# One contiguous piece per weight slab, and an identity made by GpSimd: a layer norm feeding a spectral filter and a gated MLP

## The chip, the cores and the metric

The kernel runs on one core of a Trainium2 chip. The metric is device time in microseconds (us), the median of several runs. A profile comes from one further execution; its times are counted from its first instruction. Engines are called PE or TensorE (matrix products), DVE or VectorE, ACT or ScalarE, POOL or GpSimd, and SP or SyncE, which here issues all loads and stores ("SPq" in the profile is its issuing of them).

## The reference, cut to what matters

The input x has 2048 rows of 448 columns. It is normalised by row, and three things are added: x itself, a spectral filter of the normalised rows (a two-dimensional real FFT, a product with complex weights, the inverse), and an MLP whose gate passes only where it is positive.

```python
x = A_x                                   # 1 x 2048 x 448
xn = _layernorm(x, axis=-1)
X = rfft2(xn) * (w_r + 1j * w_i);  a = irfft2(X)
gate = xn @ W_gate; up = xn @ W_up        # 448 x 1792 each
h = gate * (gate > 0) * up
return x + a + h @ W_down                 # 1792 x 448
```

## The kernel before, in words

**Precision.** Float32 operands are split into two float16 parts, hi and lo, and a product is made of three passes (hi hi, hi lo, lo hi). For that, weights are first scaled by a power of two: ScalarE sums the squares of a slab (`w_sq`, line 194), GpSimd adds over the partitions (`w_sum`, line 197), VectorE makes the scale from the exponent in two instructions (`w_scale`, lines 200 and 204), ScalarE writes the hi part (`w_hi`, line 664) and VectorE the lo part (`w_lo`, line 668).

**Tiling.** The 2048 rows are 16 blocks of 128 (n2 from 0 to 15), taken as four chunks of four blocks in the order 0, 2, 1, 3. The 1792 hidden columns are 14 tiles f of 128, in groups of 5, 5 and 4. A unit "gu" makes gate and up of one tile for one chunk (lines 714 and 721), a unit "dn" the down projection of one group for one block (line 782). A slab (f, g) is the weight of tile f for gate (g = 0) or up (g = 1): 128 partitions of 4 x 128 float32. `load_w` (line 234) loads one slab, and eight slabs have room in SBUF at a time. Before, the array in DRAM is laid out (tile, partition, gate or up, 4, 128), so that a slab is 128 rows of 2,048 bytes, 4 KB apart.

**The opening.** The first part of the order is written out by hand, in the string `OPENING` (line 30): each token stands for a piece of work, and under `tc.manual_schedule` (line 1074) every engine does its instructions in this order. `lx` and `lw` load a block of x (line 228) and the next slab; `lid` loads the identity (line 1022), `lwd` a tile of the down weights (line 244); `st` makes a block's statistics (lines 256 and 259), `sqA`/`sqB` the standard deviations (ScalarE, line 267) and `rsA`/`rsB` their inverses (VectorE, lines 272 to 277); `xn` normalises (line 294); `hi` and `lo` split (lines 301 and 323); `cp` copies columns together on GpSimd (lines 307 and 308); `tpA` and `tpB` transpose on TensorE against the identity `id_t` (line 338), and `vev`/`aev` bring the result to SBUF on VectorE (line 346) or ScalarE (line 344). `warm` and `kw` are matrix products of zeros (line 1020) that keep TensorE busy; their operand is made by a MEMSET on GpSimd (line 1077). `hh`, `lh` and `hl` are the first product passes. All loads go through SyncE's queue in the order of the string. It begins `lx0 lx4 lw lid lw lx8 lx12 lw lw lw lw lx2`.

Only the transposes of the first chunk use the identity. Those of later chunks are DMA transposes (line 332).

**Behind the opening** the order isn't written out. The program gives every unit its side work: `sched` (line 976) sets slab work so many gu units ahead of its first use, and a list of FFT pieces with costs is drawn down by `run_bg`. The costs of VectorE pieces are in `V_US` (line 1088). The framework's scheduler then orders each engine by priorities and by modelled times (`schedule_with_timeline_sim`, line 1186), with anchors (`tc.issue_after`) that hold side work behind earlier units.

**The inverse transform** needs pairs of rows swapped between partitions; this is done by two DMAs each (`swap`, lines 547 and 548), on which VectorE waits at line 553.

## Time and profile before

| | us |
|---|---|
| median of 3 runs | 448.41 |
| the runs | 447.95, 448.41, 448.84 |
| span of the profiled execution | 446.9 |

For the profiled execution no other time than its span is listed.

Rows of a timeline read: start in us, duration in us (for x4 the whole stretch of four), engine, line, operation, output <- input, shape, count, and in brackets how long the engine had been idle before and what released it. Rows of groups read: the same names, then total busy us, mean ns of one, idle time before them and its releasers. Rows of the chain of waits read: start, duration, what was on the chain. A row of the table by stretches gives the window, its length, the busy time and count of each engine, the granted TensorE clock (1.00 is full), the DMA engines' mean busy share and the rate in GB/s.

### The profile page before, as it was taken

To read this page: it belongs to the slowest core of one execution; us is meant where nothing else is said; L and a number is where in the kernel's file an instruction comes from. 1 tells how busy PE (TensorE), PEld (TensorE's weight loads), DVE (VectorE), ACT (ScalarE), POOL (GpSimd) and SP (SyncE) were. 2 spreads that over 40 slices of the span, in tenths; PEclk is the share of its full clock that TensorE was granted. 3 is DMA by queue.
4 is the path that set the end of the run, shared out by engine and by line. 5 is a ranking of instruction groups with operands and counts; after the bars stand their busy time and mean duration, and the time that the engine had idled before them with its cause. 6 is when DMAs were issued, how large, how long until landed. Compare 5 with 4: busy or idle time off the path is not lost.

```text
span 446.9 us, 7057 instructions
## 1 busy us (share of the span) xinstructions
PE 437.4 (98%) x2618; PEld 217.6 (49%) x2618; DVE 373.0 (83%) x801; ACT 178.7 (40%) x365; POOL 35.5 (8%) x100
## 2 busy tenths in 40 slices
PE   7999999999999999999999999999999999999996
PEld 2543545444545444444444444444444456546564
DVE  5988696998859989899999999896997998656474
ACT  5886242451543666043224145434142242233230
POOL 2431031040000150000000010000000000000000
PEclk9999999999999999999999999999999999999999
DMA  7919976041001261431220021000001332121113
GB/s 243 362 38 266 359 243 118 1 94 38 0 14 61 96 219 37 129 103 64 82 77 11 1 83 54 0 13 0 14 0 42 106 96 74 54 76 53 64 43 123
DMA packets 36827, 39.66 MB, mean 89 GB/s; under 512 B 17799, under 2 KB 32185, under 8 KB 36793
## 3 DMA queue, kind: packets, MB, share of 16 engines
q1 hardware_dynamic: 36792, 39.21, 28.1%
q8 instruction: 20, 0.33, 0.3%
q14 instruction: 15, 0.11, 0.1%
HBM read 24.45 MB, written 3.67 MB: 63 GB/s over the span
## 4 chain that ended last, share of the span: by engine, by line
PE 84%; DVE 7%; DMA 4%; ACT 1%; issue 1%; POOL 1%; SPq 1%; DVEq 0%; ACTq 0%
PE gu L714 47%; PE dn L782 27%; PE gu L721 3%; PE fx L360 2%; PE fx L392 2%; DMA sw<-y 2%; PE fx L611 2%; PE fx L632 1%; DMA y<-in_xr 1%; DVE g L755 1%; DMA T<-tt 1%; DVE bst L256 1%; DVE wt L668 1%; DVE xy L788 1%; DVE y L553 1%
## 5 line engine op out<-in xcount | busy, mean ns | idle before, releaser
L714 PE MATMUL gu<-T,wt 128*128 128x512 f16 (+1 forms) x1140 | 256.1, 376 | 0.0
L714 PEld LDWEIGHTS <-wt 128*128 128x128 f16 x1140 | 108.6, 98 | 129.9 <-issue 9.3
L782 PE MATMUL dn<-wdt,h 128*128 128x448 f16 x672 | 136.4, 352 | 0.0
L782 PEld LDWEIGHTS <-h 128*128 128x128 f16 x672 | 64.8, 98 | 60.5
L751 ACT ACTIVATE g<-gu 128x512 f32<-128x512 f32 x56 | 33.2, 594 | 111.0 <-PE gu L721 75.3
L759 ACT ACTIVATE h<-g 128x512 f16<-128x512 f32 x56 | 35.0, 626 | 52.8 <-DVE g L755 52.7
L755 DVE SCALAR_TENSOR_TENSOR g<-gu,g 128x512 f32<-128x512 f32 x56 | 38.3, 684 | 10.3 <-ACT g L751 10.2
L788 DVE SCALAR_TENSOR_TENSOR xy<-dn,dsc,xy 128x448 f32<-128x448 f32 x48 | 32.5, 678 | 15.5 <-PE dn L782 15.3
L763 DVE TENSOR_TENSOR h<-g,h 128x512 f16<-128x512 f32 x56 | 38.2, 684 | 4.9 <-ACT h L759 4.8
L664 ACT ACTIVATE wt<-wst,wsc 128x512 f16<-128x512 f32 x28 | 19.1, 716 | 15.7 <-DVE wsc L204 15.7
L197 POOL PARTITION_ALL_REDUCE wm<-wm x15 | 7.9, 523 | 159.2 <-ACT junk L194 159.2
L668 DVE SCALAR_TENSOR_TENSOR wt<-wst,wsc,wt 128x512 f16<-128x512 f32 x28 | 20.4, 744 | 0.0
L637 DVE SCALAR_TENSOR_TENSOR xy<-fx,fsc,xy 128x448 f32<-128x448 f32 x16 | 10.8, 679 | 10.1 <-PE fx L632 10.1
L721 PE MATMUL gu<-T,wt 64*128 64x512 f16 x112 | 17.0, 381 | 1.7 <-DVE g L755 0.8
L399 DVE TENSOR_TENSOR y<-y 128x456 f32<-128x456 f32 x22 | 13.9, 630 | 4.7 <-DMA row<-y 4.5
L194 ACT ACTIVATE junk<-wst 128x512 bf16<-128x512 f32 x28 | 17.4, 622 | 0.3
L553 DVE TENSOR_TENSOR y<-y,sw 128x456 f32<-128x456 f32 x16 | 10.0, 626 | 8.5 <-DMA sw<-y 8.5
L595 ACT ACTIVATE vt<-y,fsc 128x912 f16<-128x912 f32 x8 | 8.4, 1052 | 20.7 <-PE fx L611 12.3
L618 ACT ACTIVATE wf<-fx 114x512 f16<-114x512 f32 x16 | 9.4, 587 | 17.2 <-PE fx L611 17.0
L398 DVE TENSOR_TENSOR y<-y 128x456 f32<-128x456 f32 x22 | 13.8, 626 | 0.2
L611 PEld LDWEIGHTS <-vt 128*128 128x128 f16 x192 | 12.0, 98 | 3.3
L611 PE MATMUL fx<-wf,vt 128*128 128x128 f16 x192 | 13.2, 219 | 0.0
(115 smaller groups left out, 430.6 us busy)
## 6 DMA issues: line engine op xcount, KB each, us to landing
sw<-y SPq DMA_DIRECT2D x32, 224.4 KB
wst<-in_wgu SPq DMA_DIRECT2D x28, 256.0 KB
wf<-in_wf SPq DMA_DIRECT2D x8, 456.0 KB
y<-in_xr SPq DMA_DIRECT2D x16, 224.0 KB
xy<-in_x SPq DMA_DIRECT2D x16, 224.0 KB
out<-xy SPq DMA_DIRECT2D x16, 224.0 KB
wdst<-in_wd SPq DMA_DIRECT2D x14, 224.0 KB
fm<-in_c_fm SPq DMA_DIRECT2D x8, 128.0 KB
```

The source lines that it names most:

```text
L194: A.activation(o, src, AF.Square, scale=SQ, accum_out=acc)
L611: P.matmul(o, v[:, h, w], m[:, c, :], start=(i == 0), stop=(i == 2), skip_group_check=True)
L664: A.activation(w[:, 0:4, :], wst[f, g], AF.Copy, scale=wsc[f, g])
L668: V.scalar_tensor_tensor(w[:, 4:8, :], st, sc, w[:, 0:4, :], op0=OP.mult, op1=OP.subtract)
L714: last["P"] = P.matmul(hps[f, q][:, g, cs], wt[f, g][:, a, :], Tq[q][:, b, cs], start=(start and i == 0), stop=(stop and i == len(seq) - 1 ...
L721: m = P.matmul(hps[f, q][:, g, 0:512], wt[f, g][rows, 7, :], Tq[q][rows, b, :], start=start, stop=not start).ins
L751: last["A"] = A.activation(g1s[f, q], hps[f, q][:, 0, :], AF.Relu, scale=2.0 ** -22).ins
L755: last["V"] = V.scalar_tensor_tensor(g1, hps[f, q][:, 1, :], 2.0 ** -22, g1, op0=OP.mult, op1=OP.mult).ins
L759: A.activation(ht[f, q][:, 0, :], g1s[f, q], AF.Copy)
L763: V.tensor_tensor(h[:, 1, :], g1s.pop((f, q)), h[:, 0, :], op=OP.subtract)
L782: last["P"] = P.matmul(ps[:, 0:D], ht[f, q][:, a, js], wdt[f][:, b, :], start=(i == 0), stop=(i == n - 1)).ins
L788: last["V"] = V.scalar_tensor_tensor(xy[:, n2, :], dps[n2][:, 0:D], dsc[:, g:g + 1], xy[:, n2, :], op0=OP.mult, op1=OP.add).ins
```

## The change

Three things are changed.

1. The gate and up weights are laid out in DRAM as (tile, gate or up, partition, 4, 128), so that each slab is one piece of 256 KB. The load reads the same bytes into the same place.
2. The identity isn't loaded. GpSimd makes it: a MEMSET of zeros and an `affine_select` that writes 1 where row and column are equal. Both stand behind the MEMSET of the warm-up tile. The token `lid` leaves the string, and the input `ident` leaves the program.
3. The pieces `rs` and `wsc` of the string are cut into their single VectorE instructions (`rsA.0` to `rsA.4`, `wscW0g0.0` and `.1`, and so on). They stand next to each other where the whole pieces stood, so apart from `lid` the order is the same. In the scheduled part `w_scale` becomes `w_exp` and `w_scale`, set in the same slot one after the other.

```diff
-lx0 lx4 lw lid lw lx8 lx12 lw lw lw lw lx2 lx10 lx6 lx14 lwd0 lwd1 lwd2 lwd3 lwd4 warm st0 st4 sqA rsA hi4
+lx0 lx4 lw lw lx8 lx12 lw lw lw lw lx2 lx10 lx6 lx14 lwd0 lwd1 lwd2 lwd3 lwd4 warm st0 st4 sqA rsA.0 rsA.1 rsA.2 rsA.3 rsA.4 hi4
...
     def load_w(f, g, eng=nc.sync):
         wst[f, g] = mt([128, 4, 128], F32, "wst", 8)
-        eng.dma_start(wst[f, g], wgu[f, :, g])
+        eng.dma_start(wst[f, g], wgu[f, g])
...
+    def w_exp(f, gs=(0, 1)):
+        half_exponent(eg[:, f, gs[0]:gs[-1] + 1], state["wm", f][:, 1, gs[0]:gs[-1] + 1])
+
     def w_scale(f, gs=(0, 1)):
         sc = mt([128, 2], F32, "wsc", 6)
-        e = eg[:, f, gs[0]:gs[-1] + 1]
-        half_exponent(e, state["wm", f][:, 1, gs[0]:gs[-1] + 1])
-        shift_exponent(sc[:, 0:len(gs)], e, -1, 188)
+        shift_exponent(sc[:, 0:len(gs)], eg[:, f, gs[0]:gs[-1] + 1], -1, 188)
...
         sched(gslot(s, 7), w_sum, f)
+        sched(gslot(s, 5), w_exp, f)
         sched(gslot(s, 5), w_scale, f)
...
-    pieces = {"lid": lambda: nc.sync.dma_start(id_t, ident), "lfd": lambda: nc.sync.dma_start(fd_t, c_fd),
+    pieces = {"lfd": lambda: nc.sync.dma_start(fd_t, c_fd),
...
         G.memset(warm, 0.0)
+        G.memset(id_t, 0.0)
+        G.affine_select(id_t, id_t, pattern=[[-1, 128]], compare_op=OP.not_equal, fill=1.0, base=0, channel_multiplier=1)
         wps = psum.tile([128, 512], F32, name="dn", bufs=2)
...
-    wgu = np.ascontiguousarray(np.stack([wtiles(B_W_gate), wtiles(B_W_up)], axis=2))
+    wgu = np.ascontiguousarray(np.stack([wtiles(B_W_gate), wtiles(B_W_up)], axis=1))
```

## The prediction

> **What bounds the kernel now.** I read the page first (busy shares, DMA packets), then a table of busy time by stretch, then the opening instruction by instruction with the release of each wait.

> ```profile
> span 446.9 us, 7057 instructions
> PE 437.4 (98%) x2618; PEld 217.6 (49%) x2618; DVE 373.0 (83%) x801; ACT 178.7 (40%) x365; POOL 35.5 (8%) x100
> ```

> TensorE is busy for 437.4 of 446.9 us, so a change that leaves its work alone can win only out of the other 9.5 us. The table shows where these lie (after the window and its length come each engine's busy time with its count of instructions, then granted clock, DMA share, GB/s):

> ```profile
> 0.00:7.50 7.50, 5.92 (x19) 2.13 (x19) 3.21 (x12) 3.04 (x6) 1.35 (x11) 1.00 0.67 203
> 7.50:13.60 6.10, 3.57 (x26) 1.69 (x27) 5.47 (x22) 4.97 (x14) 2.16 (x7) 1.00 1.01 356
> 13.60:19.30 5.70, 5.54 (x56) 4.72 (x56) 5.60 (x15) 5.44 (x12) 2.28 (x7) 1.00 1.02 369
> 19.30:366.00 346.70, 345.93 (x1882) 163.77 (x1883) 308.80 (x676) 143.61 (x303) 29.75 (x76) 1.00 0.27 81
> 366.00:400.00 34.00, 33.19 (x263) 18.81 (x260) 23.02 (x39) 8.75 (x14) 0.00 (x0) 1.00 0.23 74
> 400.00:443.20 43.20, 43.20 (x378) 26.46 (x376) 26.17 (x39) 12.87 (x21) 0.00 (x0) 1.00 0.17 63
> 443.20:446.90 3.70, 0.06 (x1) 0.00 (x0) 0.68 (x1) 0.00 (x0) 0.00 (x0) 1.00 0.32 121
> ```

> From 13.6 us TensorE stands for 0.16 us to 19.3, 0.77 us to 366, 0.81 us to 400, and not at all to 443.2; then one last piece and a store take 3.7 us. The granted clock is 1.00 throughout. The kernel is an opening of 13.6 us and then TensorE's own work. Whatever makes the first product pass start earlier arrives at the end almost whole; whatever only speeds a load in the middle arrives nowhere. Everything turns on the opening, and here are its rows:

> ```profile
> 0.96 0.52 POOL L1077 MEMSET warm<- 128x512 f16 x1
> 2.14 0.43 SPq L1022 DMA_DIRECT2D id_t<-in_ident  x1
> 2.62 0.43 SPq L234 DMA_DIRECT2D wst<-in_wgu  x1
> 3.09 0.91 SPq L228 DMA_DIRECT2D y<-in_xr  x2
> 6.90 0.61 ACT L194 ACTIVATE junk<-wst 128x512 bf16<-128x512 f32 x1
> 7.06 0.22 POOL L307 COPY tt<-tt 128x48 f16<-128x48 f16 x1 [5.57 <-ACT tt L301]
> 7.51 0.74 ACT L301 ACTIVATE tt<-y,rs 128x448 f16<-128x448 f32 x1
> 7.85 0.63 DVE L256 BATCH_NORM_STATS2 bst<-y 128x6 f32<-128x448 f32 x1 [0.80 <-DMA y<-in_xr]
> 8.32 0.51 PE L338 MATMUL fx<-id_t,tt 128*128 128x128 f16 x6 [0.85 <-ACT tt L301]
> 9.46 0.29 ACT L267 ACTIVATE rs<-mv,eps 128x2 f32<-128x2 f32 x1 [0.58 <-DVE mv L259]
> 9.92 0.45 PE L338 MATMUL fx<-id_t,tt 128*128 128x128 f16 x5 [0.88 <-DVE tt L323]
> 12.03 0.45 PE L338 MATMUL fx<-id_t,tt 128*128 128x128 f16 x5 [0.36 <-DVE tt L323]
> 13.12 1.01 DVE L346 COPY T<-fx 128x384 f16<-128x384 f16 x3
> 13.62 0.33 PE L338 MATMUL fx<-id_t,tt 128*128 128x128 f16 x3 [0.48 <-ACT wt L664]
> ```

> One wait on a load stands in this chain: at 7.85 VectorE had stood 0.80 us for the third block of x (lx8). From there it is busy for 5.47 of the 6.10 us to 13.6, and TensorE and ScalarE wait for it (0.88 and 0.36 us for the low halves, 0.58 us for the statistics). The transposes themselves never wait for the identity: the first, at 8.32, was released by ScalarE's high half. And no row says that ScalarE's first sum of squares (6.90) waited for weights: it stands behind other ScalarE work.

> **The change part by part.** *The identity's load goes.* SyncE issues it at 2.14 in its order, and the next issue starts at 2.62: 0.48 us of SyncE, with the loads of W0g1, lx8, lx12 and all others behind it. The awaited lx8 is the second of these. How much earlier does it land? Two bounds, from the load's size and from the rate in the stretch in which it moves:

> ```profile
> id_t<-in_ident SPq DMA_DIRECT2D x1, 32.0 KB
> 4.00:5.00 1.00, 1.00 (x4) 0.37 (x3) 0.86 (x3) 0.07 (x1) 0.00 (x0) 1.00 0.67 164
> ```

> If the DMA engines were saturated, only the identity's bytes would go: 32.8 kB at the 203 GB/s of the first window is 0.16 us. If the pace is set by issuing, the whole slot goes: 0.48 us. From 4 to 5 us, after these issues and before lx8 has landed, the engines are busy for only 0.67 of the time at 164 GB/s, so they were short of work and not of bandwidth; that is nearer to the second bound. I take 0.45 us. The most that any earlier landing can give is the whole wait, 0.80 us: then VectorE is bound by its own order.

> Does 0.45 us pass down the chain? VectorE's pieces behind lx8 (statistics, low half, weight scale, second normalisation factor, evictions) follow each other closely, and their other inputs come from work that is not behind the load: the high half ends at 7.51 + 0.74 = 8.25, and the low half made from it is wanted by the transpose at 9.92, 0.45 earlier still over 1 us behind it. ScalarE has 0.58 us of slack at 9.46, more than 0.45. The transposes at 9.92 and 12.03 wait for VectorE and move with it, and with them the evictions at 13.12 and TensorE's start at 13.62. From there TensorE stands for so little that the shift reaches 443.2 and the last store.

> *The identity is made on GpSimd.* Two instructions more, behind the warm-up tile's MEMSET, which ends at 0.96 + 0.52 = 1.48. Their nearest rows:

> ```profile
> L313 POOL COPY tt<-tt 128x64 f16<-128x64 f16 x16 | 5.6, 349 | 0.0
> L197 POOL PARTITION_ALL_REDUCE wm<-wm x15 | 7.9, 523 | 159.2 <-ACT junk L194 159.2
> L488 POOL MEMSET sw<- 1x912 f32 x6 | 5.1, 850 | 0.2
> L284 POOL MEMSET tt<- 128x32 f16 x4 | 0.3, 124 | 0.3 <-POOLq L1178 0.3
> ```

> The MEMSET of 128 columns is a quarter of the warm-up tile's 0.52 us, so 0.13. The select has no row; it lies between a short MEMSET (0.12) and the longest mean of any GpSimd group, 0.85. I take the all-reduce's 0.52, as it too is more than a plain move. Together 0.65 us (0.25 to 0.98), from 1.48 to 2.13. GpSimd's next work is the copy at 7.06, after 5.57 us of idling: 4.93 us of cover. The warm-up matmuls wait for the MEMSET ahead of the two and do not move. Cost: nothing. If the cover were gone, the price would be the delay of the first transpose past 8.32, less the 0.43 us that TensorE would still wait before 9.92 (0.88 - 0.45).

> [...]

> *The weights lie in one piece.* The page and the tables say what each of the 28 loads does now:

> ```profile
> DMA packets 36827, 39.66 MB, mean 89 GB/s; under 512 B 17799, under 2 KB 32185, under 8 KB 36793
> wst<-in_wgu SPq DMA_DIRECT2D x28, 256.0 KB
> 13.00:14.00 1.00, 0.52 (x6) 0.39 (x6) 1.00 (x4) 1.00 (x2) 0.00 (x0) 1.00 1.06 402
> 9.12 3.60 SPq L244 DMA_DIRECT2D wdst<-in_wd  x5
> 155.05 1.01 SPq L234 DMA_DIRECT2D wst<-in_wgu  x2
> 156.50:157.50 1.00, 1.00 (x7) 0.23 (x6) 0.00 (x0) 0.17 (x2) 0.00 (x0) 1.00 0.98 367
> ```

> A load moves 128 rows of 2,048 B, now 4 KB apart, afterwards end to end. 28 x 128 = 3,584 packets of that size, with the 1,024 of the spectral weights (8 x 128 rows of 3.6 KB), make 4,608, which is the number of packets from 2 to 8 KB (36793 - 32185). So each row is one packet now. The down weights lie end to end already (rows of 1,792 B), and no packet between 2 and 8 KB is left over for them: they are not merged across partitions, so I expect the same 2,048 B packets afterwards. Nor does the pitch cost rate: from 13 to 14 us, behind their issue at 9.12, down weights move at 402 GB/s with a DMA share of 1.06; from 156.5 to 157.5 us two gate and up loads, issued at 155.05 and alone, move at 367 with a share of 0.98. Divided by the share that is 379 and 374, equal within 2%. I book nothing. Bounds: from no gain to the rest of lx8's wait, 0.80 - 0.45 = 0.35 us, as two of these loads are ahead of lx8; nothing more, as no other wait on them stands in the opening's rows.

> *The split pieces.* The normalisation factor and the scale are cut into single VectorE instructions, but the written order has them in the same sequence; only the identity's token is missing. In the scheduled part the scale's two instructions become two entries of the same slot with the same planned cost. Zero.

> The sum: 446.9 - 0.45 + 0 + 0 = 446.45 us of span. The page gives no time of its own for the profiled execution beside its span; the median of the runs, 448.41, lies 1.5 us above it, and I keep that distance: 447.96 us. What one measurement here can tell from no change is about 0.2%, 0.9 us; the forecast, -0.10%, is within it.

> **The rivals.** *Nothing arrives.* lx8 was late for a slow first transfer, not for its place in the queue, and VectorE waits as before: 448.4. For it: the DMA share from 7.5 us on is 1.01. Against it: the idle engines at 4 to 5 us.

> *The contiguous loads are faster.* The whole wait of 0.80 us goes: 447.6. For it: the early rate is 356 GB/s between 7.5 and 13.6, where weights move among others, below the later 402. Against it: the equal rates above. Still within the limit. [...]

> *The scheduled part is drawn anew, and better.* Past the opening the order on each engine is not written out: the scheduler makes it from modelled times, which change with the dropped load and the two new instructions. TensorE's 0.77 + 0.81 us could shrink, with the opening's 0.45 at most 2.0 us: 446.4, and about 447.0 for half of it.

> *The scheduled part is drawn anew, and worse.* This is the one that ends slower. Its place is the inverse transform's partition swaps between 366 and 400 us, where the chain of waits runs over VectorE and two loads:

> ```profile
> 380.45 4.33 DMA sw<-y
> 392.25 4.94 DMA sw<-y
> DVE y L553 <- DMA sw<-y: 8.5, 3, 4.3
> ```

> If a swap is issued later, behind another piece of VectorE's work, VectorE stands for a further part of such a landing, and TensorE with it once its down-projection work laid there (33.19 busy of 34.00) is used up. Half a landing, 2.3 us, less the opening's 0.45 gives 450.3; a delay of over 1.35 us on TensorE (0.45 + 0.9) makes it measurably slower. Against it: the anchors of the units are unchanged, and a uniform shift leaves an order as it is.

> *The identity comes late*, if the select took over 6.6 us (1.48 + 0.13 to 8.25): for 9 us the transpose is 2.4 us late, of which 0.43 is covered: 447.96 + 1.97 = 449.9.

> **How the numbers follow.** Forecast, the shift alone: 0.52. Nothing arrives: 0.10. Faster loads: 0.05. Drawn better: 0.18. Drawn worse: 0.12. Late identity: 0.03. Faster by over 0.2% (below 447.5) takes the better order and a little of the forecast's edge and of the faster loads: 0.21. Slower (above 449.3) takes the worse order and most of the last: 0.14. Within: 0.65. The range 446.8 to 449.2 holds the unknown costs (447.6 to 448.25 for the load's bounds), the half gain of a better order, and the small losses of a worse one, and leaves out about 2 in 10.

> **What would show it.** In the profile of the changed kernel: no id_t load; the next weight load's issue near 2.15; two more GpSimd rows that end near 2.1; the 0.80 us wait at 7.85 down to about 0.35, and TensorE's triple at 13.62 near 13.2; 2,048 B packets as before (128 under 512 B fewer) and the same rates; TensorE's standing from 13 us on near 1.7 us. It would be wrong if the wait stays, if a GpSimd row or a gap without a row reaches 7 us, or if the standing after 19 us changes by more than the opening does; the last would say that the order decides.

## The result and the profile after

The changed kernel takes 458.88 us (median of 4 runs, 458.8 to 459.55) against 448.4 us before: a ratio of 1.0236, 95% interval 1.0223 to 1.0249. The prediction was 447.96 us (446.8 to 449.2). The change costs 10.5 us.

The page of the changed kernel, its span and its first row of engines:

```profile
span 457.1 us, 7061 instructions
PE 440.8 (96%) x2618; PEld 219.2 (48%) x2618; DVE 373.4 (82%) x801; ACT 178.9 (39%) x365; POOL 36.1 (8%) x102
```

The span is 10.2 us longer, with 3.4 us more of TensorE's busy time for the same 2618 products, and two more GpSimd instructions. The table by stretches of the changed kernel (columns as before: engines' busy time and counts, granted clock, DMA share, GB/s) says where:

```profile
0.00:10.14 10.14, 7.12 (x19) 2.60 (x20) 5.36 (x18) 5.03 (x11) 1.43 (x12) 1.00 0.78 252
10.14:18.93 8.79, 0.94 (x11) 0.64 (x11) 0.37 (x4) 0.30 (x2) 1.12 (x6) 0.73 0.85 314
18.93:24.00 5.07, 5.07 (x20) 2.53 (x21) 4.67 (x18) 3.97 (x8) 2.39 (x8) 0.50 0.00 0
24.00:40.00 16.00, 15.73 (x104) 8.86 (x103) 13.72 (x37) 13.97 (x31) 3.35 (x14) 0.99 0.34 100
40.00:366.00 326.00, 324.97 (x1754) 153.65 (x1752) 288.84 (x630) 129.47 (x274) 27.77 (x67) 1.00 0.27 80
366.00:400.00 34.00, 34.00 (x257) 18.95 (x256) 28.10 (x50) 11.07 (x17) 0.00 (x0) 1.00 0.25 81
```

From 10.14 to 18.93 us hardly anything computes: TensorE 0.94 us, VectorE 0.37, ScalarE 0.30, GpSimd 1.12. Then TensorE works for 5.07 us at a granted clock of 0.50. From 24 to 400 us it stands for 0.27 + 1.03 + 0 = 1.3 us, no more than before (0.77 + 0.81 us from 19.3 to 400). Nearly the whole loss lies in the opening. Its timeline in the changed kernel (start, duration, engine, line, what, and the idle time ahead with its releaser; the lines of helpers are 3 to 10 lower than before):

```profile
0.96 0.52 POOL L1077 MEMSET warm<- 128x512 f16 x1
1.42 0.20 POOL L1078 MEMSET id_t<- 128x128 f16 x1
7.93 0.63 DVE L246 BATCH_NORM_STATS2 bst<-y 128x6 f32<-128x448 f32 x1 [0.84 <-DMA y<-in_xr]
9.81 0.28 POOL L1079 TENSOR_SCALAR_AFFINE_SELECT id_t<-id_t 128x128 f16<-128x128 f16 x1 [8.18 <-issue]
10.06 0.21 POOL L302 COPY tt<-tt 128x48 f16<-128x48 f16 x1
10.14 0.50 PE L333 MATMUL fx<-id_t,tt 128*128 128x128 f16 x6 [1.48 <-POOL id_t L1079]
18.13 0.40 POOL L187 PARTITION_ALL_REDUCE wm<-wm  x1 [7.67 <-issue]
18.41 0.28 POOL L302 COPY tt<-tt 128x48 f16<-128x48 f16 x1
18.56 0.15 DVE L190 TENSOR_SCALAR eg<-wm 128x1 uint32<-128x1 uint32 x1 [8.39 <-POOL wm L187]
18.58 0.30 POOL L303 COPY tt<-tt 128x64 f16<-128x64 f16 x1
18.93 0.29 PE L333 MATMUL fx<-id_t,tt 128*128 128x128 f16 x1 [7.85 <-POOL tt L303]
19.01 2.77 PE L1017 MATMUL dn<-warm 128*128 128x512 f16 x6
23.71 1.16 PE L710 MATMUL gu<-T,wt 128*128 128x256 f16 x6
```

The two brackets with "issue" on GpSimd are the result. The select itself takes 0.28 us, less than I had put down. But GpSimd is silent for 8.18 us ahead of it and for 7.67 us ahead of the first all-reduce, and in neither case waits for anything that the timeline shows: the select has no other producer than the MEMSET in front of it, and the sum of squares that the all-reduce reads was there at 7.46 + 0.19 = 7.65 (ScalarE, line 184). "issue" as a releaser is how a row says that time went by without a row. Everything else follows: the identity is there at 10.1 instead of ahead of 8.3, the first weight scale at 18.6 instead of near 10, the second block's columns, which GpSimd copies for the transposes, at 18.9 (18.58 + 0.30). VectorE waited 8.39 us and TensorE 7.85 us for GpSimd. In the kernel before, the second block's copy and the first weight scale read:

```profile
8.48 0.24 POOL L308 COPY tt<-tt 128x64 f16<-128x64 f16 x1
9.92 0.14 DVE L200 TENSOR_SCALAR eg<-wm 128x1 uint32<-128x1 uint32 x1
```

The timeline leaves out an entry that a view of one source line (`--source`) has: a MODIFY_POOL_CONFIG on GpSimd's sequencer (POOLq), for the line of the select and for that of the all-reduce, about where each silence begins (1.62 and 10.46 us). These rows read: line, queue, operation, count, shortest, median and longest time in ns, first and last start in us.

```profile
L1079 POOLq MODIFY_POOL_CONFIG  x2: 11/11/11, 1.6 to 1.7; - x2
L187 POOLq MODIFY_POOL_CONFIG  x2: 3/3/3, 10.7 to 10.7; - x2
```

The entry itself takes 3 to 11 ns. From 1.7 us to the select at 9.81, and from 10.7 to the all-reduce at 18.13, GpSimd has no row.

The kernel before has the second of these entries too, ahead of its first all-reduce, and yet no silence stood there; its row says that it waited 0.25 us for ScalarE's sum of squares:

```profile
L197 POOLq MODIFY_POOL_CONFIG  x2: 11/11/11, 7.5 to 7.5; - x2
7.70 0.39 POOL L197 PARTITION_ALL_REDUCE wm<-wm  x1 [0.25 <-ACT junk L194]
```

So the entry alone isn't the cost. But the trace of before already held a sign, at 7.5 us, that more goes with GpSimd's first all-reduce than its row in the timeline.

Two of the profiles below, of the layout alone and of the select that nobody reads, were taken in an execution in which TensorE was slower (spans of 1,628.8 and 1,628.7 us, and 5.20 us for the six warm-up products that took 1.46 us before); from them only rows of DMA and GpSimd are used, and such executions are left out of the times.

### The profile page after: what moved, and what is told of

It is laid out like the page before. It is cut to its first block, busy times and chain, and to the rows that moved or that the text cites. A ratio compares the mean times of both kernels' runs of the same rounds, so it can differ in the third digit from the quotient of the medians.

```text
span 457.1 us, 7061 instructions
## 1 busy us (share of the span) xinstructions
PE 440.8 (96%) x2618; PEld 219.2 (48%) x2618; DVE 373.4 (82%) x801; ACT 178.9 (39%) x365; POOL 36.1 (8%) x102
## 4 chain that ended last, share of the span: by engine, by line
PE 84%; DVE 6%; issue 5%; DMA 3%; ACT 1%; POOL 1%; SPq 0%; DVEq 0%; ACTq 0%; POOLq 0%
PE gu L710 46%; PE dn L778 26%; PE gu L717 3%; PE fx L355 2%; PE fx L387 2%; DMA sw<-y 2%; PE fx L606 2%; PE fx L627 1%; PE dn L1017 1%; DMA T<-tt 1%; DVE g L751 1%; DVE wt L664 1%; DVE xy L784 1%; DVE y L548 1%; DVE y L549 0%
## 5 line engine op out<-in xcount | busy, mean ns | idle before, releaser
L751 DVE SCALAR_TENSOR_TENSOR g<-gu,g 128x512 f32<-128x512 f32 x56 | 38.3, 684 | 10.7 <-ACT g L747 10.5
L784 DVE SCALAR_TENSOR_TENSOR xy<-dn,dsc,xy 128x448 f32<-128x448 f32 x48 | 32.5, 678 | 15.5 <-PE dn L778 15.3
L664 DVE SCALAR_TENSOR_TENSOR wt<-wst,wsc,wt 128x512 f16<-128x512 f32 x28 | 20.4, 746 | 1.3 <-ACT wt L660 1.3
L1017 PE MATMUL dn<-warm 128*128 128x512 f16 x29 | 11.8, 577 | 1.5 <-POOL warm L1077 1.5
## 6 DMA issues: line engine op xcount, KB each, us to landing
wst<-in_wgu SPq DMA_DIRECT2D x28, 256.0 KB
```

The source lines that it names most:

```text
L664: V.scalar_tensor_tensor(w[:, 4:8, :], st, sc, w[:, 0:4, :], op0=OP.mult, op1=OP.subtract)
L751: last["V"] = V.scalar_tensor_tensor(g1, hps[f, q][:, 1, :], 2.0 ** -22, g1, op0=OP.mult, op1=OP.mult).ins
L784: last["V"] = V.scalar_tensor_tensor(xy[:, n2, :], dps[n2][:, 0:D], dsc[:, g:g + 1], xy[:, n2, :], op0=OP.mult, op1=OP.add).ins
```

## The experiments

**The theory** is a guess from these rows: GpSimd works with one of two sets at a time; the select, coming first, brings a set that lacks the all-reduce; the all-reduce then brings its own again; each exchange takes about 8 us (8.18 and 7.67 in the changed kernel) in which GpSimd's queue stands, and the time has no row; a set stays from one execution to the next, so a kernel that uses only one pays nothing. That it is a set of code, as the expectations have it, no trace and no run shows; what the runs test is where the silences stand and what they cost. **The rivals:** the select's first call is slow by itself, wherever it stands; the layout of the weights carries part of the loss; the late identity carries it rather than the late all-reduce; an exchange slows all engines and not only GpSimd's queue.

**The layout alone.**

```diff
-        eng.dma_start(wst[f, g], wgu[f, :, g])
+        eng.dma_start(wst[f, g], wgu[f, g])
...
-    wgu = np.ascontiguousarray(np.stack([wtiles(B_W_gate), wtiles(B_W_up)], axis=2))
+    wgu = np.ascontiguousarray(np.stack([wtiles(B_W_gate), wtiles(B_W_up)], axis=1))
```

> The kernel before with the contiguous weight slabs alone; the identity is loaded as before. Theory (two sets of GpSimd code: the select needs one that lacks the all-reduce, and each exchange costs about 8 us): nothing here touches GpSimd, so 448.4 us within 0.9, and 2,048 B packets as before. Rival (the layout carries part of the loss): 450 us or more, with longer waits on the weight slabs.

448.3 us, ratio 0.9987 (0.9978 to 0.9996). The layout carries nothing of the loss. The ratio's interval ends just short of 1, so it may be worth up to 0.2%; where it would come from is open, and the kernel with the all-reduce first (below), which has the layout too, gives 1.000. The packets are as before: 36,792 - 32,184 = 4,608 between 2 and 8 KB.

```profile
DMA packets 36826, 39.66 MB, mean 24 GB/s; under 512 B 17798, under 2 KB 32184, under 8 KB 36792
```

**The identity alone.** The changed kernel with the two lines above turned back.

```diff
-        eng.dma_start(wst[f, g], wgu[f, g])
+        eng.dma_start(wst[f, g], wgu[f, :, g])
```

> The changed kernel with the old layout of the weights: only the identity by GpSimd (and the dropped load) is left. Theory (two sets of GpSimd code): the whole loss, 458.9 us within 1, with 8.2 us of silence on GpSimd ahead of the select and 7.7 us ahead of the first all-reduce. Rival (the layout carries part): under 457 us.

458.64 us, ratio 1.0222 (1.0203 to 1.0241): the whole loss, with 8.93 and 7.93 us of silence:

```profile
10.56 0.28 POOL L1079 TENSOR_SCALAR_AFFINE_SELECT id_t<-id_t 128x128 f16<-128x128 f16 x1 [8.93 <-issue]
19.15 0.40 POOL L187 PARTITION_ALL_REDUCE wm<-wm  x1 [7.93 <-issue]
```

The two runs part the change: the layout is out. This kernel also has the split pieces of point 3; so has the next one, and it loses nothing.

**The all-reduce first.** The changed kernel with an all-reduce of a constant ahead of the select.

```diff
         G.memset(warm, 0.0)
+        all_sum(mt([128, 1], F32, "dummy"), eps)
         G.memset(id_t, 0.0)
         G.affine_select(id_t, id_t, ...)
```

> The changed kernel with one more all-reduce, of a constant, put on GpSimd ahead of the identity's two instructions. Theory (two sets of code): the set that the all-reduce brings holds the select too, so with the reduce first neither is preceded by silence; the identity is ready near 3 us, GpSimd's copies stand at 7.1 again and the time is 448.4 us, 447.5 to 449.2. Rival (the select's first call is slow by itself, wherever it stands): 8 us of silence ahead of the select remain, GpSimd's copies come near 11 us, and the time is 450 us or more.

448.55 us, ratio 1.0001 (0.9992 to 1.001). GpSimd's rows in this kernel:

```profile
1.62 0.39 POOL L187 PARTITION_ALL_REDUCE dummy<-eps  x1
2.23 0.29 POOL L1080 TENSOR_SCALAR_AFFINE_SELECT id_t<-id_t 128x128 f16<-128x128 f16 x1
7.84 0.39 POOL L187 PARTITION_ALL_REDUCE wm<-wm  x1 [0.25 <-ACT junk L184]
```

No silence is left: an instruction more, and 10 us less. The select's first call isn't slow: behind an all-reduce it starts at 2.23, 0.08 us after its MEMSET ended (1.88 + 0.27). In the theory's words, the all-reduce's set serves the select too.

**The same two exchanged.** The same kernel with the constant's all-reduce behind the select.

```diff
         G.affine_select(id_t, id_t, ...)
+        all_sum(mt([128, 1], F32, "dummy"), eps)
```

> The changed kernel with one more all-reduce of a constant, put on GpSimd right behind the select: the same instructions as in the kernel with the reduce first, two of them exchanged. Theory (two sets of code): select first brings the poorer set, the reduce behind it the richer one, so both silences of about 8 us are paid, back to back from 1.6 to about 18 us, and the copies behind them wait too: 457 to 460 us. Rival (an early all-reduce helps wherever it stands, because it is the first call of the reduce that is slow): the second silence begins 8 us earlier and is hidden in part, 450 to 454 us.

460.34 us, ratio 1.0254 (1.0239 to 1.0269). The order of the same two instructions decides 11.6 us (460.34 against 448.72 for the kernel before in its session; with the all-reduce first, 448.55 against 448.57). Now the copies too stand behind both silences, of 9.31 and 8.79 us:

```profile
10.94 0.28 POOL L1079 TENSOR_SCALAR_AFFINE_SELECT id_t<-id_t 128x128 f16<-128x128 f16 x1 [9.31 <-issue]
20.01 0.40 POOL L187 PARTITION_ALL_REDUCE dummy<-eps  x1 [8.79 <-issue]
20.30 0.28 POOL L302 COPY tt<-tt 128x48 f16<-128x48 f16 x1
```

**No all-reduce at all.**

```diff
     def all_sum(o, i):
-        G.partition_all_reduce(o, i, 128, bass_isa.ReduceOp.add)
+        G.tensor_copy(o, i)
```

> The changed kernel with every all-reduce over the partitions replaced by a plain GpSimd copy: the sum over the partitions is left out, so the weight scales come from single partitions. Theory (two sets of code that replace each other): with the all-reduce gone only one set is ever used, it is still there from the execution before, and no silence stands on GpSimd: 446.5 to 448.5 us. Rival (the select's first call is slow by itself): 8 us of silence ahead of the select remain, the first transposes start near 10.1 instead of 8.3, and the time is 449 to 451 us.

448.22 us, ratio 0.999 (0.9981 to 1.0). The select stands at 1.70 us, right behind its MEMSET:

```profile
1.70 0.29 POOL L1079 TENSOR_SCALAR_AFFINE_SELECT id_t<-id_t 128x128 f16<-128x128 f16 x1
7.74 0.19 POOL L187 COPY wm<-wm 128x1 f32<-128x1 f32 x1 [0.21 <-ACT junk L184]
L1079 POOLq MODIFY_POOL_CONFIG  x2: 11/11/11, 1.6 to 1.6; - x2
```

This kernel still has the select's MODIFY_POOL_CONFIG, at 1.6 us, yet no silence follows it and the time is that of before. So the cost belongs neither to the select nor to its first call in an execution. The theory says: with one set in use, that set is there already.

**A select that nobody reads**, in the kernel before, whose identity is loaded.

```diff
         G.memset(warm, 0.0)
+        spare_t = ft([128, 128], F16, "spare_t")
+        G.memset(spare_t, 0.0)
+        G.affine_select(spare_t, spare_t, ...)
```

> The kernel before, identity loaded as ever, with a MEMSET and a select on a spare tile that nobody reads, put behind the warm-up MEMSET. Theory (the exchanges of GpSimd code block its queue, above all the one ahead of the first all-reduce): nearly the whole loss without any late identity, 457 to 459.5 us, first all-reduce near 18 us. Rival (the late identity carries the loss): the first transposes are on time at 8.3 and the time is 448 to 450 us.

Three runs took 457.05, 458.13 and 460.15 us, a ratio of 1.0213 (1.0185 to 1.024). 7.64 us of silence stand ahead of the unused select, 7.30 ahead of the first all-reduce:

```profile
9.27 0.28 POOL L1080 TENSOR_SCALAR_AFFINE_SELECT spare_t<-spare_t 128x128 f16<-128x128 f16 x1 [7.64 <-issue]
17.22 0.40 POOL L197 PARTITION_ALL_REDUCE wm<-wm  x1 [7.30 <-issue]
```

So the loss needs no late identity.

**A late identity alone.** The kernel before with the load of the identity moved.

```diff
-lx0 lx4 lw lid lw lx8 lx12 lw lw lw lw lx2
+lx0 lx4 lw lw lx8 lx12 lw lw lid lw lw lx2
```

> The kernel before with the identity's load moved behind the third and fourth weight slab, so that it lands near 10 us, about when the select delivered it in the changed kernel; GpSimd is untouched. It prices the late identity alone. Theory (the blocked all-reduce carries the loss): 448.5 to 450 us. Rival (the identity carries a large part): 452 us or more.

448.54 us, ratio 1.000 (0.9988 to 1.0011), with the first transposes at 10.51, later than in the changed kernel:

```profile
10.51 0.49 PE L338 MATMUL fx<-id_t,tt 128*128 128x128 f16 x6 [1.87 <-DMA id_t<-in_ident]
12.63 0.44 PE L338 MATMUL fx<-id_t,tt 128*128 128x128 f16 x5
14.30 0.81 PE L714 MATMUL gu<-T,wt 128*128 128x256 f16 x6
```

2.2 us of delay at the first transpose are 0.5 us at the first product (14.30 against 13.78 before), and not to be told from nothing at the end. The 1.48 us that the changed kernel waits for its identity are not the loss; the blocked all-reduce and copies are.

**One exchange, and from the execution before.** A small addition at the end of GpSimd's order, which by the theory needs the other set.

```diff
     run_bg(until=len(bg))
+    spare_t = mt([128, 1], F32, "spare_t")
+    G.tensor_tensor(spare_t, dsc[:, 2:3], dsc[:, 2:3], op=OP.add)
```

> The kernel before with one small GpSimd addition at the very end of GpSimd's order, on a spare tile that nobody reads; the addition needs the set of code without the all-reduce. Theory (one set is resident at a time, and it stays from one execution to the next): the exchange at the end is hidden, but the next execution begins with the wrong set, so the first all-reduce comes after about 8 us of silence, near 15.5 instead of 7.7, and the time is 454 to 457 us; the exchange behind the first select is so priced alone. Rival (each execution begins with its sets afresh, or a set is only loaded at its first call): the opening is as before, 448.4 us.

455.87 us, ratio 1.0167 (1.0151 to 1.0182). The addition runs at 331 us, and what it costs stands at the beginning:

```profile
331.17 0.19 POOL L1142 TENSOR_TENSOR spare_t<-dsc 128x1 f32<-128x1 f32 x1 [8.38 <-DVE wds L690]
7.27 0.24 POOL L308 COPY tt<-tt 128x64 f16<-128x64 f16 x1
15.29 0.40 POOL L197 PARTITION_ALL_REDUCE wm<-wm  x1 [7.79 <-issue]
```

Nothing in the opening was changed, and yet its first all-reduce comes 7.6 us later (15.29 against 7.70), behind 7.79 us of silence. The addition runs 316 us after it, so what delays the all-reduce was left by the execution before; in the theory's words, the wrong set. This also prices one exchange in this place: 7.2 us of the total (455.87 against 448.7 in the same session), where both in the changed kernel cost 10.5.

**Both exchanges where GpSimd is idle.** The same addition reading the second group's scale, so that it stands in the middle, with all-reduces behind it.

```diff
+    G.tensor_tensor(spare_t, dsc[:, 1:2], dsc[:, 1:2], op=OP.add)
```

> The kernel before with the same small addition in the middle, after the second group's down weights are scaled, where GpSimd has little to do; all-reduces follow, so both exchanges are paid, and the execution ends with the set that the next one begins with. Theory (an exchange costs only what waits behind it on GpSimd): both are hidden, 448.4 us within 0.9, with silences of 7 to 9 us on GpSimd ahead of the addition and ahead of the next all-reduce. Rival (an exchange costs the other engines about 8 us wherever it stands, by its traffic or by stopping the core): 456 us or more.

448.86 us, ratio 1.0008 (0.9999 to 1.0017). No bracket with "issue" shows the two exchanges, though I had expected one: the addition and the next all-reduce end waits of 23.82 and 53.32 us for other engines, each longer than any silence seen here (7.3 to 9.3 us). Their MODIFY_POOL_CONFIG rows stand at 167.7 and 192.2 us, 24 and 53 us ahead of them:

```profile
191.64 0.32 POOL L1142 TENSOR_TENSOR spare_t<-dsc 128x1 f32<-128x1 f32 x1 [23.82 <-DVE wds L690]
245.28 0.41 POOL L197 PARTITION_ALL_REDUCE wm<-wm  x1 [53.32 <-ACT junk L194]
L1142 POOLq MODIFY_POOL_CONFIG  x2: 85/85/85, 167.7 to 167.7; - x2
L197 POOLq MODIFY_POOL_CONFIG  x2: 5/5/5, 192.2 to 192.2; - x2
```

So in these runs an exchange cost what waited behind it on GpSimd: 7.2 us ahead of the opening's first all-reduce, and nothing measurable here, though no row shows when these two took place.

**The identity's load behind lx8.** For the term of the prediction: the load's slot ahead of the third block of x.

```diff
-lx0 lx4 lw lid lw lx8 lx12 lw lw lw lw lx2
+lx0 lx4 lw lw lx8 lx12 lid lw lw lw lw lx2
```

> The kernel before with the identity's load moved behind lx8 and lx12 in SyncE's order; nothing else. By the prediction's term (the slot of 0.48 us ahead of lx8 delays it): the third block of x is at hand near 7.4 instead of 7.85, 447.96 us, a ratio of 0.999. Rival (the load costs lx8 nothing, the wait is due to the first transfers): ratio 1.000 and lx8 as before.

448.37 us, ratio 0.9992 (0.9983 to 1.0001): undecided between the two. VectorE began with lx8 at 7.63, but this moment scatters by more than the term: over the executions profiled here it lay between 7.11 and 8.24 with the load ahead of lx8 (five kernels, mean 7.74), and between 7.43 and 8.33 without (seven kernels, mean 7.71). The test isn't clean either: the first transposes now waited 1.22 us for the identity, to 8.43 instead of 8.32.

**The blocks of x ahead of the second slab**, with the all-reduce first, and with the identity loaded.

```diff
-lx0 lx4 lw lw lx8 lx12 lw lw lw lw lx2
+lx0 lx4 lw lx8 lx12 lw lw lw lw lw lx2
```

> The changed kernel with the constant all-reduce ahead of the identity's instructions, and with lx8 and lx12 issued ahead of the second weight slab. If VectorE's wait for lx8 is the opening's last wait for a load, it goes (up to 0.8 us) and the start of the products moves with it: 447.7 to 448.2 us, ratio 0.998 to 0.9995. Rival (the second slab comes late in its turn and ScalarE waits for it at 8.2): ratio 1.000 or more.

448.22 us, ratio 0.9989 (0.998 to 0.9998).

```diff
-lx0 lx4 lw lid lw lx8 lx12 lw lw lw lw lx2
+lx0 lx4 lw lid lx8 lx12 lw lw lw lw lw lx2
```

> The kernel before, identity loaded and old layout, with lx8 and lx12 issued ahead of the second weight slab. If the order of the loads alone gives what the kernel with the reduce first and this order gave (ratio 0.9989), it is 0.998 to 0.9995 here too. Rival (dropping the identity's load was needed for it): ratio 1.000.

447.96 us, ratio 0.9983 (0.9974 to 0.9992). Neither the identity by GpSimd nor the layout is needed for it. In this kernel's profiled execution VectorE's wait for lx8 is gone and the first product starts 0.41 us earlier than before:

```profile
7.04 0.62 DVE L256 BATCH_NORM_STATS2 bst<-y 128x6 f32<-128x448 f32 x1
13.37 0.82 PE L714 MATMUL gu<-T,wt 128*128 128x256 f16 x6
```

This is the lowest time measured, ahead of the kernel before by 0.1 to 0.3%; the intervals of the layout alone (0.9987) and of the kernel above (0.9989) overlap with it.

## Why the prediction was wrong

**The step that failed** is the price of the identity on GpSimd: "Together 0.65 us (0.25 to 0.98)" and "4.93 us of cover. ... Cost: nothing." The two instructions took 0.20 + 0.28 us, together less than estimated. What was put at nothing is the time between instructions: 8.18 us of silence ahead of the select and 7.67 us ahead of the first all-reduce. The cover was used up at 7.06, and the all-reduce came at 18.13 instead of 7.70. I bounded the select by rows of other instructions, and a row gives the time of the instruction (0.28 us for the select), not that of the silence ahead of it (8.18 us). A select had no row in the trace of before, so no row gave it an upper bound. The prediction's own sign of being wrong, a gap without a row that reaches 7 us, came: it runs from 1.62 to 9.81.

**The rival that came nearest** was the late identity, with a chance of 0.03 and its price drawn up for the wrong work. I asked when TensorE needs the identity (8.32). I didn't price what stands in GpSimd's queue behind the select: the copies for the transposes and the all-reduce for the first weight scale, for which TensorE and VectorE then waited 7.85 and 8.39 us. A late identity of 2.2 us cost nothing measurable. The select of 9 us in that rival was a guess that no row backs: the select took 0.28 us, behind 8.18 us of silence. And I weighed one long time; there are two, the second of 7.67 us ahead of the all-reduce. Over the profiles a silence takes 7.3 to 9.3 us, and the changed kernel pays in every execution measured: its four runs took 458.8 to 459.55 us. In the kernel without all-reduces the select's first call in an execution, at 1.70, is preceded by nothing.

**The sum from the rows.** In the kernel before, the six warm-up products ahead of the first product passes, and the first of these:

```profile
10.21 1.46 PE L1020 MATMUL dn<-warm 128*128 128x512 f16 x6
13.78 0.81 PE L714 MATMUL gu<-T,wt 128*128 128x256 f16 x6
```

In the changed kernel they start at 19.01 and 23.71. So 8.80 us are lost up to the warm-up products, by the two silences, of which GpSimd's former idle time to 7.06 hid a part. Another 1.13 us are lost from there to the first product (4.70 against 3.57 us): behind 7.85 us without work TensorE's granted clock was 0.50 from 18.93 to 24.00 (1.00 throughout before), and the same six products took 2.77 instead of 1.46 us. Together 9.93 of the 10.2 us by which the spans differ.

**The identity's load, 0.45 us:** not borne out. In the changed kernel VectorE waits 0.84 us for lx8, against 0.80; moving the load alone gives 0.9992 (0.9983 to 1.0001). The kernel with the all-reduce first has no such load and no silence: it gives 1.0001 (0.9992 to 1.001), where the term asked for 0.9990. Dropping the load was worth less than can be measured, or nothing. That the wait itself is worth something was right: with lx8 issued ahead of a whole slab it goes, and 0.1 to 0.2% with it.

**The layout, nothing:** right as to the packets, and within 0.2% as to the time.

**The split pieces, zero, and the two rivals of a new order (0.30 together):** the programs' lists of instructions hold the same instructions in the same order on TensorE, VectorE and ScalarE, from the first to the last; on SyncE only the identity is missing. The 0.30 went to something that did not come about; the argument against it, that a uniform shift leaves an order as it is, held.

**The opening decides, and a shift there arrives whole:** right for the large shift: 9.93 us at the first product are 10.2 at the end. For shifts under 1 us the runs don't show it: with the late identity 0.52 us at the first product left the span 0.1 us longer (447.0), and with the blocks of x ahead 0.41 us made it 1.0 us shorter (445.9).

## What to carry to other kernels

The row of an instruction on GpSimd that the kernel has not used so far is not its whole price: here a select of 0.28 us cost 10.5 us, with 8.18 us of silence ahead of it and 7.67 us ahead of the all-reduce that followed. So look at what else GpSimd runs, and try the two in both orders: with the all-reduce first there was no silence, and the order of the same two instructions decided 11.6 us. In these traces a MODIFY_POOL_CONFIG in the view of a source line stood where each silence of the changed kernel began, at 1.7 and 10.7 us; it stood too where none followed, at 7.5 us before. If a silence can't be avoided, put it where nothing waits in GpSimd's queue (448.86 us here, against 448.7), and count the one of the next execution: 7.2 us for an addition at 331 us. When work is moved to an idle engine, ask what stands behind it in that engine's queue, not only who reads its result.
